# A new order table for 3779 steps on five engines: attention with exponential features, then a cosine feed-forward layer

## The chip, the core and the metric

The kernel runs on one core of a Trainium2 chip. The metric is the device time of one execution in microseconds (us). Engines are named as the profile names them: PE is TensorE (matmuls), PEld its weight loads, ACT is ScalarE, DVE is VectorE, POOL is GpSimd, SP is the queue that issues the transfers. L912 is line 912 of the kernel.

## The reference, cut to what matters

```python
def phi(x):                                   # q, k: 8 x 8 x 576 x 64; w_phi: 64 x 128
    proj = einsum('bhsd,df->bhsf', x, w_phi)
    proj = proj - max(abs(proj), axis=-1)
    return concatenate([exp(proj), exp(-proj)], axis=-1)
q_p, k_p = phi(q), phi(k)
kv  = einsum('bhsf,bhsd->bhfd', k_p, v);  z = sum(k_p, axis=2)
x   = einsum('bhsf,bhfd->bhsd', q_p, kv) / (einsum('bhsf,bhf->bhs', q_p, z)[..., None] + 1e-6)
h   = x.reshape(4608, 512) @ w_in             # w_in: 512 x 2048
out = (h * cos(h)) @ w_out                    # w_out: 2048 x 512
```

## The kernel before, in words

**Attention** (`attention`, L526) runs in 32 units, each of two heads. A unit projects q (L555, and L558 for the last 64 rows of both heads) and k (L601, L626) on PE. For q, ACT copies the result to SBUF (L566, L568), DVE takes the maximum over 32 x 32 blocks (L572, L580, L581), POOL spreads it (L586), DVE turns it back (L590), POOL subtracts (L594) and ACT takes the exponentials (L665). For k, DVE takes the maximum from PSUM (L639); in most units DVE negates it (L642) and ACT takes the exponentials with it as a bias (L659, eight instructions for a full half, two for the last rows); in the first units PE subtracts the maximum with one more matmul (L647), and ACT needs two instructions only (L656). PE then forms kv and z together (L705, L711), ACT copies them (L717), PE multiplies with the features of q (L740, L746), DVE divides (L752 to L767) and turns the result (L771), and SP stores it to DRAM (L781 the first 512 columns in four transfers, L777 the last 64). The turned tile `xt` has two buffers, so the turn of a unit waits until both stores of the unit two before it have landed.

**The feed-forward layer** (`visit`, L802) works on nine chunks of 512 tokens. A visit loads x (L825), splits it into a high and a low part (L49 on ACT, L54 on DVE) and forms, for a pair of 128 x 512 tiles of h at a time, x @ w_in on PE. Visits up to the ninth do this plainly (L960, 12 matmuls to a tile). Later ones use seven block products in place of eight (L912), with their sums made by DVE and ACT (L847, L924, L939, L943). From h on, the chain is the same: ACT copies out of PSUM (L967, L968) or scales (L982), DVE reduces the angle (L986), ACT takes the cosine (L990), DVE multiplies (L993), ACT and DVE split into high and low (L49, L54), and PE multiplies with w_out (L1009, L1010, L1011, three matmuls for a block of 128 tokens). The results leave through L1049, L1058, L1060 and the stores of L1069.

**The weights** (`convert`, L393) come as 64-bit words. For each of eight pairs of row blocks, ACT and DVE convert them early in the run (L415 to L462, and L49 and L54 for the parts), DVE makes four sums of blocks for the seven-product scheme in the same conversion (L470), and SP stores the parts to DRAM (L480), from where later visits load them again (L516). Exponentials and cosines need different tables on ACT, so each change between them stands as an ACT_TABLE_LOAD.

**What sets the order.** Every piece of work is a `Step` (L68) with an engine and a function that issues its instructions. There are 3779 of them: 958 on PE, 1040 on ACT, 1233 on DVE, 160 on POOL, 388 on SP. The list `ORDER` (L87) holds the numbers of all steps, and `plan` (L302) walks it once: the steps are issued in that order, each engine gets its own in that order, and the eight PSUM banks are given out on the way (a step that needs a bank takes the one whose last user stands earliest). An engine works its queue strictly in that order. A step waits for the steps that it depends on and for the last users of the bank or buffer that it takes over; the tables of costs (L85, L300) play no part any more when the kernel is issued.

Of the kernel before, what the change touches and what calls it, by code (L numbers as in the profile page):

```python
# [25 lines left out]
def phi_attention_then_cos_ffn(ctx: ExitStack, tc: tile.TileContext, qkT, vS, w_phi, w_in, w_out, out):  # L26
# [41 lines left out]
    class Step:  # L68
# [19 lines left out]
        0, 42, 1, 3, 1265, 2, 4, 5, 7, 44, 6, 8, 9, 59, 46, 17, 64, 10, 65, 11, 18, 19, 58, 68, 83, 23, 47, 24,  # L88
        43, 12, 27, 45, 20, 48, 124, 1266, 21, 16, 60, 22, 13, 62, 61, 14, 50, 25, 1267, 63, 26, 15, 49, 86, 30,
        28, 1268, 31, 66, 1269, 99, 1270, 67, 32, 51, 71, 1271, 84, 33, 29, 1284, 72, 103, 52, 1272, 73, 53, 85,  # L90
        140, 1273, 87, 88, 104, 57, 101, 89, 1280, 1281, 142, 100, 56, 102, 125, 108, 90, 165, 55, 141, 91, 143,
        107, 54, 144, 35, 74, 105, 69, 146, 1274, 1275, 34, 147, 1276, 106, 112, 92, 109, 1277, 70, 93, 36, 113,
        37, 38, 1278, 114, 94, 126, 150, 148, 181, 1279, 128, 127, 145, 39, 95, 129, 130, 185, 98, 182, 40, 75,
        149, 183, 97, 131, 76, 1285, 96, 132, 206, 166, 187, 153, 188, 133, 77, 134, 154, 111, 78, 1286, 115,
        168, 1287, 184, 110, 186, 79, 191, 1295, 1288, 167, 135, 222, 169, 247, 41, 170, 1289, 116, 171, 189,
        155, 137, 224, 117, 226, 156, 138, 190, 172, 136, 223, 80, 227, 1290, 139, 118, 81, 225, 151, 173, 209,
        174, 194, 152, 119, 175, 228, 207, 229, 1291, 195, 232, 230, 196, 120, 208, 1292, 248, 231, 263, 1506,
        210, 176, 288, 212, 157, 211, 1296, 213, 179, 158, 121, 178, 265, 235, 122, 177, 1511, 159, 160, 180,
        264, 192, 214, 236, 82, 1512, 237, 197, 269, 193, 215, 266, 289, 267, 216, 123, 161, 238, 1505, 268,
        271, 270, 217, 1507, 249, 272, 1297, 304, 251, 162, 219, 252, 250, 218, 306, 305, 163, 198, 253, 273,  # L100
        307, 221, 254, 1509, 199, 255, 220, 1513, 329, 233, 308, 276, 310, 311, 256, 234, 277, 1510, 200, 257,
        278, 314, 309, 1514, 1508, 312, 290, 201, 330, 1298, 240, 1299, 292, 1314, 239, 1300, 1515, 345, 293,
        1516, 279, 313, 1301, 291, 1517, 368, 347, 258, 1302, 294, 317, 348, 1303, 1518, 318, 353, 259, 202,
        349, 319, 260, 1528, 1304, 296, 261, 274, 350, 203, 262, 320, 354, 241, 204, 346, 1305, 385, 1537, 1519,
        242, 275, 1306, 164, 351, 1307, 352, 1529, 295, 384, 297, 355, 243, 298, 1538, 390, 332, 386, 331, 1530,
        1308, 244, 281, 1539, 245, 280, 387, 1309, 1531, 333, 299, 407, 335, 334, 358, 205, 1293, 1540, 336,
        303, 1520, 388, 1315, 300, 282, 283, 302, 1546, 1564, 337, 1312, 301, 246, 284, 369, 1521, 1310, 338,
        316, 285, 339, 1316, 315, 1541, 1317, 392, 1318, 370, 1319, 1522, 371, 372, 321, 389, 446, 391, 1523,
        373, 1563, 374, 322, 340, 287, 393, 286, 375, 424, 344, 1524, 323, 1547, 341, 1325, 376, 343, 324, 1320,
        423, 429, 325, 342, 394, 326, 357, 397, 377, 327, 1321, 1569, 356, 425, 378, 427, 359, 409, 1532, 1542,  # L110
        1567, 428, 1322, 398, 1525, 411, 410, 412, 1543, 1526, 1566, 1533, 430, 1565, 1548, 413, 361, 447, 432,
        1534, 1283, 1570, 485, 360, 1294, 379, 1527, 362, 383, 1535, 363, 1549, 415, 380, 1573, 1536, 1550,
        1326, 414, 382, 364, 1544, 381, 1574, 1551, 463, 1571, 1545, 1552, 468, 1572, 1553, 469, 1568, 433, 395,
        416, 426, 1554, 365, 417, 396, 1327, 1575, 1328, 1559, 472, 1560, 1329, 431, 1282, 1330, 448, 1331,
        1576, 462, 1561, 450, 502, 451, 466, 1562, 449, 1586, 408, 1577, 328, 467, 418, 366, 1578, 452, 1555,
        421, 454, 1332, 1344, 400, 1557, 524, 419, 367, 1587, 464, 420, 399, 1311, 453, 422, 436, 507, 1333,
        1621, 434, 1324, 1588, 435, 1334, 488, 1595, 1335, 465, 401, 471, 455, 508, 1336, 402, 456, 1337, 511,
        403, 487, 437, 457, 1596, 501, 489, 1579, 438, 470, 404, 459, 439, 505, 458, 405, 503, 460, 490, 475,
        440, 1338, 461, 441, 563, 442, 1323, 473, 504, 1339, 491, 527, 474, 486, 1604, 506, 493, 406, 443, 1580,
        1622, 492, 476, 444, 509, 1597, 494, 478, 1581, 1558, 495, 510, 477, 496, 540, 1605, 498, 526, 542, 500,  # L120
        479, 514, 1623, 480, 499, 1342, 481, 1598, 497, 482, 1589, 1599, 483, 528, 1582, 1590, 1627, 1606, 1583,
        515, 1591, 543, 541, 1556, 1584, 530, 1607, 1592, 1585, 1625, 546, 1608, 1593, 1600, 544, 1609, 545,
        1601, 529, 1594, 1624, 1345, 1626, 445, 532, 525, 1602, 564, 531, 1610, 1629, 1603, 1346, 1631, 547,
# [1027 lines left out]
```

## Time and profile before

| | us |
|---|---|
| three runs | 1038.51, 1039.48, 1040.59 |
| median | 1039.48 |
| the profiled execution, its own time | 1037.65 |
| its span (first to last instruction) | 1035.9 |
| PE busy in it | 1026.4 |
| ACT busy | 790.0 |
| DVE busy | 742.9 |

The time of an execution holds the span and some 1.75 us around it (1037.65 - 1035.9). The profiled execution lies 1.83 us below the median of the three runs. A view of the profile in windows gives the busy time of each engine between two marks, in us from the start of the span; the columns after the engines are the TensorE clock that was granted (1.00 is full), the share of the transfer engines that was busy, and GB/s. In the timeline a row gives the start, the length, the engine, the line and how many instructions are merged in it, and in square brackets how long the engine was idle just before and what ended that. Matmuls overlap, so the pitch of two rows is read from their starts. A step of fp32 data shows twice as many matmuls as the program issues.

### The profile page before, as it was taken

Reading aid. Unit: us, or ns where it says so; the run is one execution under the profiler, and the core shown is the slowest. Engines: PE = TensorE matmul, PEld = TensorE weight load, DVE = VectorE, ACT = ScalarE, POOL = GpSimd, SP = SyncE. Lnnn points to the kernel's source line nnn. Section 1 sums busy time; section 2 is a strip of 40 time slices with the busy share of each in tenths; the row PEclk is TensorE's granted clock in tenths of the full one; section 3 lists DMA queues with packets and bytes.
Section 4 is the critical chain, followed back from the end, with each engine's and each line's share of the span. In section 5 each row is a group of like instructions: output and inputs, shape, how many; then the busy total and the mean of one; then the engine's idle time right before and its main releaser. Section 6 shows DMA issues by size and latency. Waiting matters only on the chain.

```text
span 1035.9 us, 24223 instructions
## 1 busy us (share of the span) xinstructions
PE 1026.4 (99%) x9738; PEld 883.3 (85%) x9738; DVE 742.9 (72%) x1426; ACT 790.0 (76%) x1634; POOL 147.7 (14%) x231
## 2 busy tenths in 40 slices
PE   9998999999999999999999999999999999999998
PEld 6786788888878888988889898888899989989897
DVE  7998998999898877766677457686556475466544
ACT  6999999898777778787789958887778555455543
POOL 3342242201101001201112011132001000000000
PEclk9999999999999999999999999999999999999999
DMA  7676587247677644687336761567317655752852
GB/s 250 189 217 203 169 261 244 100 159 247 225 246 269 203 147 163 210 277 288 115 111 222 254 230 67 185 235 260 153 55 277 213 157 182 265 180 96 284 193 92
DMA packets 88768, 204.44 MB, mean 197 GB/s; under 512 B 20688, under 2 KB 42320, under 8 KB 84816
## 3 DMA queue, kind: packets, MB, share of 16 engines
q1 hardware_dynamic: 88512, 202.83, 57.9%
q8 instruction: 76, 1.25, 0.5%
q14 instruction: 36, 0.29, 0.1%
q10 hardware_dynamic: 144, 0.07, 0.0%
HBM read 154.63 MB, written 48.23 MB: 196 GB/s over the span
## 4 chain that ended last, share of the span: by engine, by line
PE 95%; DVE 3%; issue 1%; DMA 0%; SPq 0%; ACT 0%; DVEq 0%
PE bank L912 23%; PE bank L1009 13%; PE bank L1010 12%; PE bank L1011 12%; PE bank L960 12%; PE bank L705 6%; PE bank L740 6%; PE bank L555 3%; PE bank L601 3%; PE bank L711 1%; PE bank L647 1%; PE bank L558 1%; PE bank L626 1%; PE bank L746 1%; DMA wo_parts<-wo 0%
## 5 line engine op out<-in xcount | busy, mean ns | idle before, releaser
L1009 PE MATMUL bank<-wo,gh 128*128 128x512 f32 x576 | 229.5, 399 | 0.0
L1010 PE MATMUL bank<-wo,gh 128*128 128x512 f32 x576 | 225.3, 391 | 0.0
L1011 PE MATMUL bank<-wo,gl 128*128 128x512 f32 x576 | 224.6, 390 | 0.0
L924 ACT ACTIVATE hs<-bank 128x256 f32<-128x256 f32 x192 | 71.2, 389 | 92.7 <-PE bank L912 81.7
L594 POOL TENSOR_TENSOR pq<-pq,bq 128x288 f32<-128x288 f32 x128 | 114.2, 923 | 172.1 <-DVE bq L590 121.5
L986 DVE SCALAR_TENSOR_TENSOR g<-g,hs 128x512 f32<-128x512 int32 x144 | 98.2, 689 | 50.7 <-ACT g L982 47.6
L659 ACT ACTIVATE ek<-bank,mk 128x128 f32<-128x128 f32 x464 | 128.3, 420 | 5.4 <-DVE mk L642 5.1
L54 DVE TENSOR_TENSOR gl<-g,gh 128x512 fp32r<-128x512 f32 x144 | 100.4, 701 | 40.7 <-ACT gh L49 39.4
L1011 PEld LDWEIGHTS bank<-wo,gl 128*128 128x128 f32 x576 | 108.2, 188 | 23.8
L1009 PEld LDWEIGHTS bank<-wo,gh 128*128 128x128 f32 x576 | 108.4, 188 | 23.3 <-issue 2.2
L990 ACT ACTIVATE g<-g,halfpi 128x512 f32<-128x512 f32 x144 | 101.4, 719 | 30.4 <-DVE g L986 29.9
L912 PE MATMUL bank<-xh_t,wi 128*128 128x256 f32 x768 | 124.0, 284 | 0.4 <-issue 0.4
L1010 PEld LDWEIGHTS bank<-wo,gh 128*128 128x128 f32 x576 | 108.6, 188 | 18.2
L993 DVE TENSOR_TENSOR g<-hs,g 128x512 f32<-128x512 f32 x144 | 97.6, 689 | 31.7 <-ACT g L990 31.3
L49 ACT ACTIVATE gh<-g 128x512 fp32r<-128x512 f32 x144 | 91.5, 641 | 31.2 <-DVE g L993 16.2
L912 PEld LDWEIGHTS bank<-xh_t,wi 128*128 128x128 f32 x768 | 109.4, 191 | 6.4 <-issue 1.2
L586 POOL COPY m<-m 32x36 f32<-32x36 f32 x96 | 32.7, 341 | 469.4 <-DVE m L581 445.4
L912 PE MATMUL bank<-xh_b,wi 128*128 128x256 f32 x576 | 93.3, 284 | 0.0
L665 ACT ACTIVATE eq<-pq 128x576 f32<-128x576 f32 x128 | 81.3, 716 | 4.0 <-PE bank L740 2.5
L912 PEld LDWEIGHTS bank<-xh_b,wi 128*128 128x128 f32 x576 | 81.0, 191 | 2.8 <-issue 0.2
L982 ACT ACTIVATE g<-hs 128x512 int32<-128x512 f32 x96 | 60.2, 638 | 24.5 <-DVE hs L939 18.9
L912 PE MATMUL bank<-xl_t,wi 128*128 128x256 f32 x384 | 77.3, 283 | 0.0
(93 smaller groups left out, 1803.4 us busy)
## 6 DMA issues: line engine op xcount, KB each, us to landing
wi<-wi_parts SPq DMA_DIRECT2D x30, 1792.0 KB, 8.3
wo<-wo_parts SPq DMA_DIRECT2D x30, 1024.0 KB, 5.5
qk<-qkT SPq DMA_DIRECT2D x31, 640.0 KB, 5.3
x_raw<-xs SPq DMA_DIRECT2D x47, 256.0 KB, 4.8
vs<-vS SPq DMA_DIRECT2D x32, 325.0 KB, 4.8
wi_raw<-w_in SPq DMA_DIRECT2D x8, 1024.0 KB, 6.1
wo_raw<-w_out SPq DMA_DIRECT2D x8, 1024.0 KB, 6.2
xs<-xt SPq DMA_DIRECT2D x128, 64.0 KB, 3.4
```

Source lines behind the costliest of these rows:

```text
L49: ACT.activation(out=out, in_=in_, func=AF.Copy, scale=1.0)
L54: eng.tensor_tensor(out=out, in0=in_, in1=hi.bitcast(F32), op=ALU.subtract)
L594: qeng.tensor_tensor(out=d["pq"][:, c], in0=d["pq"][:, c], in1=d["bq"][:, c], op=ALU.subtract)
L659: ACT.activation(out=e[:, g, s * P:(s + 1) * P], in_=pk[:, g, :], func=AF.Exp, scale=1.0 - 2.0 * s, bias=d["lk" if s == 0 else "mk", i][:, ...
L912: PE.matmul(out=out, lhsT=w[:, part, block, j * P:(j + 1) * P], rhs=d[x, name][:, j * HC:(j + 1) * HC], start=start and k == 0, stop=k == ...
L960: PE.matmul(out=bank(b), lhsT=w[:, part, 2 * r + kt // 2, kt % 2 * P:(kt % 2 + 1) * P], rhs=d.get(("from", kt), d)[x, kt], start=(k == 0), ...
L986: DVE.scalar_tensor_tensor(out=g, in0=g.bitcast(I32), scalar=-TWO_PI, in1=m["hs", r], op0=ALU.mult, op1=ALU.add)
L990: ACT.activation(out=n["g"], in_=n["g"], func=AF.Sin, bias=halfpi, scale=1.0)
L993: DVE.tensor_tensor(out=n["g"], in0=m["hs", r], in1=n["g"], op=ALU.mult)
L1009: PE.matmul(out=a, lhsT=gh[:, t], rhs=w[:, 0, r], start=first, stop=False)
L1010: PE.matmul(out=a, lhsT=gh[:, t], rhs=w[:, 1, r], start=False, stop=False)
L1011: PE.matmul(out=a, lhsT=gl[:, t], rhs=w[:, 0, r], start=False, stop=last)
```

## The change

The change replaces the list `ORDER`. The list of steps, their functions, their dependencies and their buffers are the same; the new list holds the same 3779 numbers, and 3669 of its places hold another number than before. By the words that came with it, the table is from a search over four sets of transfer landing times at once; the sums of weight blocks in the conversions (L470), which these words name as well, stand in both kernels. Since banks are given out along the list, many steps use another PSUM bank than before.

```diff
     ORDER = [
-        0, 42, 1, 3, 1265, 2, 4, 5, 7, 44, 6, 8, 9, 59, 46, 17, 64, 10, 65, 11, 18, 19, 58, 68, 83, 23, 47, 24,
+        0, 4, 3, 5, 7, 8, 42, 6, 1, 44, 17, 18, 9, 45, 59, 1265, 46, 2, 10, 19, 23, 20, 58, 24, 47, 11, 12, 27,
...
-        3765, 3759, 3766, 3767, 3770, 3768, 3772, 3771, 3769, 3774, 3773, 3776, 3775, 3777, 3778,
+        3770, 3768, 3771, 3773, 3774, 3769, 3776, 3777, 3775, 3778,
     ]
```

Two places show what moves. The first is the DVE queue at the start of the program, before the change and after it; `mk` is the maximum of k over a bank, `m` and `bq` that of q. Before:

```order
L572 TENSOR_REDUCE m_127<-pq 128x18 x2
L639 TENSOR_REDUCE mk<-bank_74 128x1
L580 TENSOR_TENSOR m_150<-m_127 64x36
L581 TENSOR_TENSOR m_151<-m_150 32x36
L642 TENSOR_SCALAR mk<-mk 128x1
L639 TENSOR_REDUCE mk<-bank_75 128x4
L639 TENSOR_REDUCE mk<-bank_69 128x1
L642 TENSOR_SCALAR mk<-mk 128x1
L590 STREAM_TRANSPOSE bq<-m_151 128x1152
L639 TENSOR_REDUCE mk<-bank_76 128x4
```

And after:

```order
L572 TENSOR_REDUCE m_121<-pq 128x18 x2
L580 TENSOR_TENSOR m_150<-m_121 64x36
L581 TENSOR_TENSOR m_151<-m_150 32x36
L639 TENSOR_REDUCE mk<-bank_74 128x4
L639 TENSOR_REDUCE mk<-bank_76 128x1
L642 TENSOR_SCALAR mk<-mk 128x1
L590 STREAM_TRANSPOSE bq<-m_151 128x1152
L639 TENSOR_REDUCE mk<-bank_75 128x4
L639 TENSOR_REDUCE mk<-bank_69 128x1
```

The long transpose of L590 stood between the second and the third full maximum of k (banks 75 and 76 before); it now stands between the first and the second of them (banks 74 and 75).

PE takes up these maxima with L647, whose rows at the same place read, before:

```order
L558 MATMUL bank_72<-qk,wphi 128x128
L647 MATMUL bank_75<-mk,minus 128x512
L647 MATMUL bank_76<-mk,minus 128x512
L647 MATMUL bank_71<-mk,minus 128x512
L647 MATMUL bank_70<-mk,minus 128x512
```

And after:

```order
L647 MATMUL bank_74<-mk,minus 128x512
L601 MATMUL bank_71<-wphi,qk 128x128
L601 MATMUL bank_72<-wphi,qk 128x128
L601 MATMUL bank_71<-wphi,qk 128x128
L601 MATMUL bank_72<-wphi,qk 128x128
L601 MATMUL bank_71<-wphi,qk 128x128
L601 MATMUL bank_72<-wphi,qk 128x128
L601 MATMUL bank_71<-wphi,qk 128x128
L601 MATMUL bank_72<-wphi,qk 128x128
L647 MATMUL bank_75<-mk,minus 128x512
```

One whole projection of k (eight matmuls of L601) now stands between the first and the second of these subtractions, where the first two followed each other.

The third place is the SP queue near 85 us, in the stretch where attention, conversions and the first visits overlap. The numbers behind `xt` tell the units apart: xt_1308 before and xt_1250 after are the turned tile of one and the same unit, xt_1397 and xt_1372 that of the next. Before:

```order
L781 DMA xs_77<-xt_1308 32x4x128 x4
L777 DMA xs_tail_78<-xt_993 128x64
L781 DMA xs_77<-xt_1397 32x4x128 x4
L537 DMA qk_1448<-qkT 128x1280
L777 DMA xs_tail_78<-xt_1308 128x64
L480 DMA wo_parts0_98<-wo_728 128x1024
L825 DMA x_raw_1522<-xs_77 128x512
L480 DMA wi_parts1_91<-wi_1228 128x1024
L777 DMA xs_tail_78<-xt_1397 128x64
```

And after:

```order
L537 DMA qk_1378<-qkT 128x1280
L480 DMA wi_parts0_90<-wi_321 128x768
L777 DMA xs_tail_78<-xt_1250 128x64
L541 DMA vs1_89<-vS 128x650
L781 DMA xs_77<-xt_1250 32x4x128 x4
L480 DMA wi_parts0_90<-wi_321 128x768
L781 DMA xs_77<-xt_1372 32x4x128 x4
L480 DMA wi_parts1_91<-wi_1231 128x1024
L777 DMA xs_tail_78<-xt_1372 128x64
```

The last of the two stores that free a buffer of `xt` (xs_tail of xt_1308) stood behind the store of the next unit's tile; now both stores of a tile (xt_1250) stand ahead of it, and a load of v stands between them.

418 rows, old and new, of the table ORDER are left out of this document.

## Prediction

> **What bounds the kernel now.** I read the page first, then busy time by windows, then PE's waits, then the timeline where PE waits. The page gives the span and the engines:
>
> ```profile
> span 1035.9 us, 24223 instructions
> PE 1026.4 (99%) x9738; PEld 883.3 (85%) x9738; DVE 742.9 (72%) x1426; ACT 790.0 (76%) x1634; POOL 147.7 (14%) x231
> ```
>
> PE is busy for 1026.4 of 1035.9 us, and no step is added or taken away. An order can win only in the 9.5 us between, or where PE is busy but slow. The windows say where these lie:
>
> ```profile
> 0.00:66.00 66.00, 64.65 (x1092) 49.37 (x1092) 57.45 (x126) 54.95 (x109) 28.03 (x51) 1.00 0.70 221
> 66.00:113.00 47.00, 43.27 (x645) 33.97 (x642) 43.95 (x98) 45.43 (x114) 14.19 (x23) 0.96 0.62 191
> 113.00:165.00 52.00, 51.87 (x636) 42.78 (x635) 49.32 (x111) 51.84 (x111) 16.70 (x27) 1.00 0.69 221
> 165.00:400.00 235.00, 235.00 (x1575) 192.54 (x1574) 201.74 (x324) 197.31 (x357) 28.82 (x37) 1.00 0.62 208
> 400.00:1036.00 636.00, 631.60 (x5799) 564.61 (x5798) 390.42 (x770) 440.43 (x948) 59.96 (x95) 1.00 0.55 189
> ```
>
> After the lengths come PE, PEld, DVE and ACT. From 165 us to the end PE is idle for 4.4 us in all, most of it the last stores. From 66 to 113 us it is idle for 3.7 us, the granted clock is 0.96, and ACT is busy for 45.43 of 47 us. That is the one stretch with something to win. PE's waits name who ended them:
>
> ```profile
> PE bank L740 <- ACT ek L659: 2.7, 1, 2.7
> ...
> PE bank L705 <- ACT pq L566: 0.5, 1, 0.5
> ...
> PE bank L647 <- DVE mk L639: 0.2, 1, 0.2
> ```
>
> The largest is one pause ended by the exponentials of k on ACT. No transfer stands in PE's list: loads are hidden behind work, in 165 us and later as well. The pause in PE's timeline, and the clock after it (windows, TensorE clock third from the end):
>
> ```profile
> 94.16 0.49 PE L558 MATMUL bank<-qk,wphi 128*128 128x128 f32 x2
> 97.39 3.60 PE L740 MATMUL bank<-kv,eq 128*64 128x65 f32 x64 [2.75 <-ACT ek L659]
> ...
> 97.00:98.00 1.00, 0.61 (x14) 0.61 (x16) 0.97 (x2) 1.00 (x4) 0.00 (x0) 0.79 0.99 390
> 98.00:99.00 1.00, 1.00 (x24) 1.00 (x22) 0.90 (x2) 1.00 (x3) 0.00 (x0) 0.50 1.09 444
> 99.00:100.00 1.00, 1.00 (x24) 1.00 (x22) 1.00 (x4) 0.22 (x1) 0.00 (x0) 0.50 0.98 403
> 100.00:101.00 1.00, 1.00 (x25) 1.00 (x23) 1.00 (x2) 1.00 (x5) 0.00 (x0) 0.50 1.11 378
> ```
>
> Behind a pause of 2.75 us the clock fell to one half for some 3.4 us, which costs PE 0.21 + 3 x 0.5 = 1.7 us more. [...]
>
> **Term 1, the stretch that ACT limits.** From the end of one tile of h (L960) to the first matmul that waits for the last exponentials of this stretch, before has:
>
> ```profile
> 73.70:112.50 38.80, 35.10 (x534) 27.68 (x533) 35.85 (x86) 37.91 (x91) 13.27 (x21) 0.96 0.57 174
> ```
>
> ACT works 37.91 of 38.80 us: PE's loss here is ACT's work less PE's. PE is idle for 3.70 us and loses 1.7 to the clock, so its own work is about 38.80 - 3.70 - 1.7 = 33.4 us. In the new order the same kind of stretch, with the same last exponentials at its end, begins one step group earlier, at a projection of q (L555) that frees ACT. Counted from the two orders, ACT has in it the same groups as before and one half of exponentials of k (eight L659) and one weight part (L49, 128x1024) more, and one x part (L49, 128x512) less. PE has one tile of L960 and one step of L740 with L746 more, and three matmuls of L1009 to L1011 less. Pitches of these, from the starts of neighbouring rows:
>
> ```profile
> 78.33 2.23 ACT L659 ACTIVATE ek<-bank,mk 128x128 f32<-128x128 f32 x8
> 80.33 1.38 ACT L665 ACTIVATE eq<-pq 128x576 f32<-128x576 f32 x2
> ...
> 72.52 1.13 ACT L49 ACTIVATE wi<-wi_t 128x1024 fp32r<-128x1024 f32 x1
> 73.47 0.34 ACT L568 ACTIVATE pq<-bank 128x128 f32<-128x128 f32 x1
> ...
> 105.34 0.70 ACT L49 ACTIVATE xh_t<-x_raw 128x512 fp32r<-128x512 f32 x1
> 105.86 1.32 ACT L665 ACTIVATE eq<-pq 128x576 f32<-128x576 f32 x2
> ```
>
> ```profile
> 67.14 1.15 PE L740 MATMUL bank<-kv,eq 128*64 128x65 f32 x32
> 68.35 1.10 PE L740 MATMUL bank<-kv,eq 128*64 128x65 f32 x32
> ...
> 70.96 2.76 PE bank L960 x12
> ...
> 1022.30 0.39 PE L1009 MATMUL bank<-wo,gh 128*128 128x512 f32 x1
> 1022.98 0.39 PE L1009 MATMUL bank<-wo,gh 128*128 128x512 f32 x1
> ```
>
> ACT: 2.00 + 0.95 - 0.52 = 2.43 us more. PE: 2.76 + 1.21 - 0.68 = 3.29 us more. PE has 0.86 us more to do while it waits for ACT, so the loss falls by 0.9. The bounds: nothing, if these steps stand where PE waits anyway, and 1.8 us, if ACT's own idle time (38.80 - 37.91 = 0.89) goes too.
>
> **Term 2, ACT's idle time in that stretch.** Its cause can be followed on DVE, SP and ACT:
>
> ```profile
> 94.52 0.78 DVE L771 STREAM_TRANSPOSE xt<-rb 128x576 f32<-128x576 f32 x1 [1.55 <-DMA wo_parts<-wo]
> ...
> 85.55 3.43 SPq L781 DMA_DIRECT2D xs<-xt  x4
> 89.08 0.39 SPq L537 DMA_DIRECT2D qk<-qkT  x1
> 89.52 0.45 SPq L777 DMA_DIRECT2D xs_tail<-xt  x1
> ...
> 99.78 2.17 ACT L659 ACTIVATE ek<-bank,mk 128x128 f32<-128x128 f32 x8 [0.78 <-DVE mk L642]
> ```
>
> DVE stood 1.55 us before a turn (L771) until a transfer landed. That transfer must be a store that frees a buffer of `xt`: the xs_tail of two units back, which left SP only at 89.52, behind the four stores of the next tile, and 5 us before DVE went on. (The row names a weight store issued beside it.) DVE's delay then kept ACT waiting for 0.78 us, for L642. In the new order both stores of a tile stand ahead of the next tile's, so that they no longer wait for its turn. What they wait for instead is a load of v, queued ahead of one of them, which needs its buffer back from an earlier L705; that step stands one group of L601 (0.98), two steps of L740 (1.21 each) and one tile of L960 (2.76), over 6 us of PE work, ahead of the turn. So this wait should go, worth 0 to 0.8 us. In the same stretch two other halves of exponentials now stand closer behind their L642 on DVE than any did before, and can make ACT wait in turn. I take half: 0.4 us less.
>
> **Term 3, the start.** Between the first two full maxima of k DVE now has L639 for the tail, L642 and the transpose L590; PE has one projection (L601) and one L647 between the two matmuls that use these maxima.
>
> ```profile
> L590 DVE STREAM_TRANSPOSE bq<-m 128x1152 f32<-128x1152 f32 x32 | 43.8, 1368 | 1.8 <-POOL m L586 1.8
> L639 DVE TENSOR_REDUCE mk<-bank 128x4 f32<-128x512 f32 (+1 forms) x96 | 50.7, 543 | 14.7 <-PE bank L626 6.6 <-PE bank L601 5.7 <-ACT g L990 2.4
> ...
> 21.04 1.13 PE L555 MATMUL bank<-qk,wphi 64*128 64x512 f32 x4
> 22.00 1.06 PE L601 MATMUL bank<-wphi,qk 64*128 64x128 f32 x16
> 22.98 1.13 PE L647 MATMUL bank<-mk,minus 128*128 128x512 f32 x2
> 23.95 0.27 PE L626 MATMUL bank<-wphi,qk 128*128 128x128 f32 x1
> ```
>
> DVE needs about 1.37 + 0.54 plus some 0.3 for the small ones, 2.2 us; PE has 0.98 + 0.97, 1.95 us. PE waits 0.25 us longer here, and the old wait of 0.2 us for L639 stands where it did or goes: between 0.5 us lost and 0.2 won, I take 0.3 lost.
>
> **Term 4, changes of shape on PE.** PE's matmuls use the whole array, its upper rows (L555, L601: 64 rows) or half its columns (L705 to L746). From L555 to L601, both of the upper rows, the pitch is 0.96 us (21.04 to 22.00). From L555 to L740 it is 67.14 less the start of this row:
>
> ```profile
> 66.08 1.13 PE L555 MATMUL bank<-qk,wphi 64*128 64x512 f32 x4
> ```
>
> That is 1.06 us, so a change of shape costs 0.10 us. Counted from the orders there are 151 such changes before and 156 after: 0.5 us lost. With other pairs of neighbours it can be 0 to 1.5.
>
> **Term 5, the rest.** From 165 us on PE waits for nothing that the list shows, and the new order leaves the chains from L912 to L1009 as long in PE work as they were, except at the very end: behind the last L912 the new order has 8 double groups of L1009 to L1011 before the last tile's, where there were 10. Their 16 x 0.68 = 10.9 us of PE work now cover 12 single instructions of DVE (none longer than the 0.78 us of L771, 9.4 us at most) and the ACT instructions between them. That is cover still; for a wait in it I take 0.2 us lost, between 0 and 0.8.
>
> **The sum.** -0.9 - 0.4 + 0.3 + 0.5 + 0.2 = -0.3 us. Against the profiled execution that is 1037.65 - 0.3 = 1037.35; the median of the runs lies 1.83 above it, so 1039.2 us for the median. About 0.2% (2.1 us) is what a measurement of this kernel can tell from no change; this is none.
>
> **Rivals.**
>
> *Faster: the stretch falls to ACT's floor.* Term 1 then gives 1.8 us with ACT's idle time in it, the start wait of 0.2 goes, and the changes of shape cost nothing more: 1.8 + 0.2 and 0.5 more if PE's own 33.4 us shrink where it need not start again behind a wait: 2.5 us, 1037.0. For it speaks that the cause of DVE's wait is moved, and that, by the same counts and pitches, PE falls behind ACT by about 1 us at each of five places in the new order and not by 2.75 at one, so the clock may stay whole. Against it: ACT, not PE, limits that stretch, so a whole clock mostly buys waiting. Chance 0.30.
>
> *Slower: the half clock on the path.* The new stretch ends with L740 waiting for eight L659, and behind it ACT's lead over PE grows again. A pause at that place as long as 2.75 us would halve the clock when PE is the limit, and its 1.7 us would not be hidden behind ACT. With Term 2 at nothing, and 0.8 at the end: -0.9 + 1.7 + 0.3 + 0.5 + 0.8 = +2.4, 1041.9. It decides at the length of the longest pause: some 2.7 us does it, as above; five pauses of 1 us don't. [...] Chance 0.23.
>
> *Nothing moves.* The terms cancel within 2.1 us: my forecast, 0.47.
>
> **How the numbers follow.** The range takes in 1037.0 and 1041.9 with 0.8 to 0.9 us around them for the bounds of Terms 3 to 5: 1036.2 to 1042.8. Faster 0.30, within 0.2% 0.47, slower 0.23.
>
> **What would show it.** Right: PE idle 2 to 4 us between 66 and 113 us, ACT busy there above 95%, no wait of DVE's L771 on a transfer near 94 us, PE's wait for L639 0.3 to 0.6 us in all, nothing new after 165 us. A window at half clock behind a pause under 2 us, or waits of PE after 165 us of over 1 us, above all for a transfer (loads of wi or wo landing late), would make it wrong.

## The result, and the profile after

The new table is slower. The median of the kernel after is 1046.15 us (6 executions, 1042.82 to 1048.23) against 1038.47 us before (6 executions, 1037.48 to 1040.59): a ratio of 1.0072, 95% interval 1.0052 to 1.0092, some 7.5 us. The prediction was 1039.2 us in a range of 1036.2 to 1042.8. The profiled execution of after was its fastest, 1042.82 us with a span of 1041.1 us and a granted clock of 1.000; the five others had a clock of .998 or .996. That spread, 5.4 us against 3.1 before, belongs to the result. One execution in experiment 2 took 1439.68 us at a granted clock of .655 and is left out of its median.

The page gives PE 1026.9 us of 1041.1: PE is idle for 14.2 us, where it was 9.5. So 4.7 of the 5.2 us between the two spans are waits. Before's 1026.4 us of work held 1.7 us of half clock that this execution of after has not, so at full clock PE's own work grew as well, by some 2.2 us (1026.9 - 1026.4 + 1.7); 4.7 + 2.2 - 1.7 gives the 5.2. The same windows as for before (lengths, then PE, PEld, DVE, ACT, POOL, TensorE clock, DMA):

```profile
66.00:113.00 47.00, 42.26 (x675) 33.88 (x671) 44.51 (x101) 45.91 (x114) 14.95 (x25) 1.00 0.69 220
113.00:165.00 52.00, 51.65 (x633) 42.62 (x632) 47.69 (x104) 50.82 (x110) 16.34 (x25) 1.00 0.56 174
165.00:400.00 235.00, 234.27 (x1572) 192.12 (x1571) 205.80 (x325) 198.88 (x354) 31.99 (x35) 1.00 0.61 208
400.00:1036.00 636.00, 633.57 (x5802) 564.71 (x5801) 392.36 (x776) 442.16 (x952) 59.34 (x98) 1.00 0.55 191
```

From 66 to 113 us PE is now idle for 4.74 us instead of 3.73, but at full clock; before lost 1.7 us to half clock there. Between 165 and 400 us, where PE had no idle time at all, it has 0.73. PE's list of waits names the largest loss:

```profile
PE bank L912 <- DMA wi<-wi_parts: 2.2, 1, 2.2
PE bank L740 <- ACT pq L566: 1.4, 1, 1.4
...
PE bank L1009 <- ACT ek L659: 0.9, 1, 0.9
PE bank L647 <- DVE mk L639: 0.8, 1, 0.8
PE bank L601 <- ACT pq L566: 0.7, 1, 0.7
PE bank L740 <- ACT ek L659: 0.7, 1, 0.7
PE bank L740 <- ACT kv L717: 0.6, 1, 0.6
```

There is one long wait, and it is for a transfer; PE's list in before had no wait for a transfer. Below it the one pause of 2.7 us for ACT has become several of 0.5 to 1.4. PE's timeline at the long one:

```profile
832.69 0.39 PE L1011 MATMUL bank<-wo,gl 128*128 128x512 f32 x1
835.29 0.74 PE L912 MATMUL bank<-xh_b,wi 128*128 128x256 f32 x4 [2.21 <-DMA wi<-wi_parts]
```

PE stops at the first use of weights that step 3131 loads (a reload of wi, L516). What SP did ahead of that load, in after's timeline of SP (start, length, issuing line):

```profile
807.68 0.32 SPq L516 DMA_DIRECT2D wo<-wo_parts  x1
808.05 0.53 SPq L516 DMA_DIRECT2D wi<-wi_parts  x1
808.63 9.55 SPq L781 DMA_DIRECT2D xs<-xt  x8
818.22 9.29 SPq L834 DMA_DIRECT2D x_raw<-xs_tail  x16
827.62 0.52 SPq L516 DMA_DIRECT2D wi<-wi_parts  x1
```

and the same load in before:

```profile
806.35 0.52 SPq L516 DMA_DIRECT2D wi<-wi_parts  x1
806.93 9.01 SPq L834 DMA_DIRECT2D x_raw<-xs_tail  x8
816.09 0.52 SPq L516 DMA_DIRECT2D wi<-wi_parts  x1
```

PE's first use of that load in before:

```profile
829.66 0.65 PE L912 MATMUL bank<-xh_b,wi 128*128 128x256 f32 x4
```

Between the two wi loads before had 8 transfers, after has 24: eight stores and sixteen loads, 18.8 us of SP's time. The load goes out at 827.62 instead of 816.09 us. By the trace's landing times it landed at 835.25 us, and PE goes on at 835.29; in before it landed at 825.79 and was first used at 829.66, 3.9 us later. SP's own waits between 800 and 840 us say why the eight stores took 9.55 us:

```profile
SPq L516 <- PE bank L1011: 7.6, 1, 7.6
SPq L781 <- DMA wi<-wi_parts: 5.1, 1, 5.1
```

First the wo load stood 7.6 us at the head of the queue, until PE gave its buffer back. Then the eighth transfer behind the first wi load had to wait 5.1 us until that load had landed: every transfer signals its landing on one of eight semaphores, which the program uses in turn, and each one waits until the transfer before it on its semaphore has landed (smallest distance 0.02 us; last section).

**The theory (T).** One reload of weights, queued too late on SP, lands in the microsecond of its first use. The wait varies from execution to execution, and when it is long enough, half clock follows. **Rivals.** R1: the spread and the loss come from the stretch to 113 us, through half clock there. R2: other work, longer chains or new waits elsewhere. R3: all of it lies behind 685 us. Later forecasts add R4 (the DMA engines, not the queue), G (PE's idle time brings half clock), and S and C for what is left once the load is early (the front of the program, or chains behind it).

### The profile page after: what moved, and what is told of

Its sections match the earlier page's. It is cut to its first block, busy times and chain, and to the rows that moved or that the text cites. A ratio compares the mean times of both kernels' runs of the same rounds, so it can differ in the third digit from the quotient of the medians.

```text
span 1041.1 us, 24198 instructions
## 1 busy us (share of the span) xinstructions
PE 1026.9 (99%) x9738; PEld 881.6 (85%) x9738; DVE 749.1 (72%) x1426; ACT 792.5 (76%) x1636; POOL 148.5 (14%) x231
## 4 chain that ended last, share of the span: by engine, by line
PE 82%; DVE 7%; ACT 6%; DMA 2%; issue 1%; SPq 1%; DVEq 0%; ACTq 0%
PE bank L912 22%; PE bank L1009 12%; PE bank L1011 12%; PE bank L1010 11%; PE bank L960 9%; PE bank L705 4%; PE bank L740 4%; PE bank L601 2%; PE bank L555 2%; ACT ek L659 2%; DMA xs<-xt 1%; PE bank L647 1%; PE bank L711 1%; ACT eq L665 1%; DMA wi<-wi_parts 1%
## 5 line engine op out<-in xcount | busy, mean ns | idle before, releaser
L1009 PE MATMUL bank<-wo,gh 128*128 128x512 f32 x576 | 229.8, 399 | 0.9 <-ACT ek L659 0.9
L1009 PEld LDWEIGHTS bank<-wo,gh 128*128 128x128 f32 x576 | 108.5, 188 | 25.1 <-issue 3.2
L912 PE MATMUL bank<-xh_t,wi 128*128 128x256 f32 x768 | 124.6, 285 | 0.2 <-ACT ek L659 0.2
L993 DVE TENSOR_TENSOR g<-hs,g 128x512 f32<-128x512 f32 x144 | 99.6, 697 | 26.0 <-ACT g L990 25.7
L912 PEld LDWEIGHTS bank<-xh_t,wi 128*128 128x128 f32 x768 | 108.7, 191 | 7.1 <-ACT hs L924 1.2
L912 PE MATMUL bank<-xh_b,wi 128*128 128x256 f32 x576 | 93.8, 285 | 2.2 <-DMA wi<-wi_parts 2.2
L912 PEld LDWEIGHTS bank<-xh_b,wi 128*128 128x128 f32 x576 | 81.0, 191 | 6.2 <-DMA wi<-wi_parts 2.6
L912 PE MATMUL bank<-xl_t,wi 128*128 128x256 f32 x384 | 77.3, 283 | 0.0
L740 PEld LDWEIGHTS bank<-kv,eq 128*64 128x64 f32 x2048 | 64.5, 138 | 13.1 <-ACT pq L566 3.0
```

What stands on the lines that cost most here:

```text
L740: PE.matmul(out=ps[64 * h:64 * h + 64, 65 * g:65 * g + 65], lhsT=d["eq", j][:, n, c:c + 64], rhs=d["kv"][:, 2 * n + j, :], start=h not in ...
L912: PE.matmul(out=out, lhsT=w[:, part, block, j * P:(j + 1) * P], rhs=d[x, name][:, j * HC:(j + 1) * HC], start=start and k == 0, stop=k == ...
L993: DVE.tensor_tensor(out=n["g"], in0=m["hs", r], in1=n["g"], op=ALU.mult)
L1009: PE.matmul(out=a, lhsT=gh[:, t], rhs=w[:, 0, r], start=first, stop=False)
```

## The experiments

All were compared with before on the same chip; "ratio" is to before.

**1. The kernel after, again**, no edit.

> The kernel after, unchanged, for more executions and a second trace. Its profiled execution (span 1041.1 us, time 1042.82, granted clock 1.000) was the fastest of six; the other five, at 1045.77 to 1048.23 us, had a granted clock of .996 or .998. Theory T (late loads): the wi load of step 3131, queued on SP behind 24 other transfers, lands in the microsecond of its first use; in slow executions PE waits there for over the 2.2 us of the profiled one, and half clock follows. A trace at 1045 to 1048 us then shows a PE wait of 3 us or more for wi or wo at 700 to 1005 us, with a half-clock window behind it. Rival R1 (spread from the ACT-limited stretch): it shows the half clock between 85 and 112 us, behind a PE pause for ACT, and the transfer wait at 835 us stays near 2.2. Rival R2 (other work): no half clock, and the time lies spread over PE's steps. Median by all: 1044 to 1048 us.

Median 1045.70 us (6 executions, 1042.65 to 1047.54), ratio 1.0066 (1.0051 to 1.0081). The profiled execution took 1045.65. PE's row at the place, and the windows behind it (PE, PEld, DVE, ACT, POOL, clock):

```profile
836.65 0.74 PE L912 MATMUL bank<-xh_b,wi 128*128 128x256 f32 x4 [3.57 <-DMA wi<-wi_parts]
```

```profile
837.00:838.00 1.00, 1.00 (x8) 1.00 (x7) 0.00 (x0) 0.00 (x0) 0.00 (x0) 0.65 0.94 359
838.00:839.00 1.00, 1.00 (x7) 1.00 (x6) 0.00 (x0) 0.00 (x0) 0.00 (x0) 0.50 0.87 237
```

All other waits are within 0.1 us of those of the first trace. The wait for wi is 3.57 instead of 2.21 us, the clock is one half from 837.30 on for 3.41 us, and the span is 1043.9 instead of 1041.1 us: 1.36 + 1.7 = 3.1 us come from this one place, a little more than the 2.8 us between the spans. That is T's picture. R1 does not show: there is no half clock in the stretch to 113 us in either trace of after. Of these six executions the two with clocks of .999 and 1.000 are the two shortest, 1043.07 and 1042.65.

**2. The same load earlier.** Two versions: four stores behind the previous wi load, and directly behind it.

```
-    ]
+    ]; ORDER.remove(3131); ORDER.insert(ORDER.index(1146) + 1, 3131)
```

```
-    ]
+    ]; ORDER.remove(3131); ORDER.insert(ORDER.index(3100) + 1, 3131)
```

> The kernel after with one DMA issue moved: the wi load of step 3131 right behind the store of step 1146, 20 transfers earlier on SP. T: the PE wait at 835 us (2.2 us in the profiled execution) is gone; a fast execution has a span of 1038.5 to 1039.5 us, and the median falls by 2.2 to 5 us, to 1041 to 1044 us, as the half clock behind that wait goes with it. R1: the fastest execution falls by 2.2 us, but the median by no more (about 1044), since half clock still comes in the stretch to 112 us. R2: the wait is replaced by another of its size; median 1045 to 1047.

> The kernel after with the wi load of step 3131 at the first place that its buffer allows, right behind the wi load of step 3100; SP then waits there some 5 us for the buffer, and the 8 stores and 16 loads behind it go out later. T: no PE wait for wi at 835 us, as with the load four stores further down (1043.5 us median, 1041.6 lowest). The trace of that one held a PE pause of 1.95 us at 75 us that the profile puts down to no wait, with half clock behind it; after's own traces have none. If that pause comes by chance, it is absent here or in part of the executions, and the lowest time is 1039.5 to 1040.5 us; if it belongs to these programs, lowest 1041.5. Rival: the stores and loads held back make a new wait, 1043 to 1046.

The first: median 1043.48 us (5 executions, 1041.56 to 1044.02), ratio 1.0041 (1.0028 to 1.0054). The second: 1041.31 us (5 executions, 1040.94 to 1044.29), ratio 1.0046 (1.0034 to 1.0059). The wait for wi is gone in both; in the second, SP issues both wi loads together and then the rest:

```profile
809.04 5.84 SPq L516 DMA_DIRECT2D wi<-wi_parts  x2
814.93 8.95 SPq L781 DMA_DIRECT2D xs<-xt  x8
823.92 8.05 SPq L834 DMA_DIRECT2D x_raw<-xs_tail  x16
```

The load now lands some 9 us (first version) and 10 us (second) before its first use, and the stores and loads held back make no new wait of its size. With the two runs of after at 1.0072 and 1.0066, moving one DMA issue is worth about 0.0026, 2.7 us, in both versions alike. (The two were measured on different chips, so the ratios are compared and not the medians.) T had said 2.2 to 5 us; the fastest span of the first version, 1039.8 us, lies just above its 1038.5 to 1039.5. R2 falls for this part of the loss: no other wait takes the place. R1 does not fall as clearly: beside experiment 1, on the same chip, the first version's median is lower by 2.2 us and, with 1043.48, near R1's 1044. Its trace has half clock in the stretch to 113 us too, but not behind a pause for ACT: the pause stands in the middle of a run of 64 matmuls, and after's two traces did not have it.

```profile
75.49 0.57 PE L705 MATMUL bank<-vs,ek 128*64 128x65 f32 x11 [1.95 <-issue]
```

The second has it too, with 1.13 us and no half clock behind it; its lowest time, 1040.94 us, lies between the forecasts for a pause by chance and for one in every execution. The pause is taken up at the end.

**3. The same load later, in the kernel before.** The other direction: before with step 3131 moved behind the wo load of step 3070.

```
-    ]
+    ]; ORDER.remove(3131); ORDER.insert(ORDER.index(3070) + 1, 3131)
```

> The kernel before with the same wi load (step 3131) put late: right behind the wo load of step 3070, that is behind a store and eight x loads. It then issues at about 824 to 827 us instead of 816.1, lands 8 to 9.5 us later, and its first use stood at 829.7 us. T: PE waits 2.5 to 6 us there for wi, with half clock behind it when over about 2.7, and the median is 1041 to 1046 us (2.5 to 7.5 over before). R1 and R2 have the price of a late load at its wait alone, with nothing behind it: 1040.5 to 1042. If the load takes less time with fewer transfers ahead of it, no wait: 1038.5.

Median 1045.15 us (5 executions, 1044.04 to 1045.19), ratio 1.0062 (1.005 to 1.0074), in T's range and above the 1040.5 to 1042 of R1 and R2. One moved DMA issue makes before as slow as after. SP, then PE:

```profile
818.71 4.55 SPq L834 DMA_DIRECT2D x_raw<-xs_tail  x8
825.48 0.34 SPq L516 DMA_DIRECT2D wo<-wo_parts  x1
825.86 0.52 SPq L516 DMA_DIRECT2D wi<-wi_parts  x1
```

```profile
835.59 0.77 PE L912 MATMUL bank<-xh_b,wi 128*128 128x256 f32 x2 [4.89 <-DMA wi<-wi_parts]
```

The load goes out at 825.86, lands at 835.45 us, and PE waits 4.89 us with half clock from 835.34 on. 4.89 + 1.7 = 6.6 us, against 6.4 us between the medians (elsewhere this execution lost 1.7 us at 72 us to a late load of x, and had no half clock near 97 us, which saved as much). T is shown in both directions.

**4. All 60 reloads at the first place that their buffers allow**, right behind the last user of the buffer.

```
-    ]
+    ]; [(ORDER.remove(a), ORDER.insert(ORDER.index(b) + 1, a)) for a, b in ((2185, 2165), (2216, 2198),
...
+    (3649, 3616), (3618, 3647), (3680, 3678))]
```

> The kernel after with all 60 reloads of wi and wo issued right behind the last user of their buffer, as the kernel before has nearly all of them; every other step in the order of after. T: no PE wait for a transfer is left behind 400 us, executions agree within 2 us, and the median is 1039.5 to 1041.5 us: after's own 1042.8 less 2.2, and what is left over 1038.5 are shape changes (+0.8) and steps behind 165 us (about +2) less 1.3 in the ACT-limited stretch. R1: the spread stays, median 1043 to 1045. R2: loads at their earliest place delay stores and loads of x behind them on SP; new PE waits for x, median 1044 to 1047.

Median 1083.47 us (6 executions, 1078.81 to 1089.23), ratio 1.0434: 45 us slower than before and 37 slower than after. All three forecasts missed. "Earlier" is not the remedy. PE's waits, and SP's:

```profile
PE bank L1011 <- DVE gl L54: 7.8, 2, 7.4
PE bank L1009 <- DVE o L1049: 7.8, 1, 7.8
PE bank L555 <- DMA qk<-qkT: 3.9, 1, 3.9
PE bank L740 <- DVE o L1060: 3.4, 1, 3.4
```

```profile
SPq L516 <- PE bank L912: 189.2, 25, 18.0
SPq L516 <- PE bank L1011: 166.0, 23, 13.3
```

The same two rows of SP in after:

```profile
SPq L516 <- PE bank L912: 126.3, 19, 18.0
SPq L516 <- PE bank L1011: 118.6, 16, 13.3
```

SP issues in the table's order. A reload at the head of its queue waits for PE to give the buffer back, and everything behind it waits too: 355 us of such waits instead of 245. The sum alone does not make a kernel slow: before has 261 us of it. What counts is what stands behind the waiting load. Stores of o, loads of qk and of v then come late, and PE waits for those. Of the rivals R2 named this mechanism (new waits behind held-back transfers) but not its size. Half clock came on top, 27.3 us of it in all, 13.7 us lost (a granted clock of .987 over 1083.1 us). Counted from the two orders, before has no other SP step between the last user of the buffer and the reload in 44 of 60 cases, after in 15. So before issues most of its reloads as early as this and is the faster table: early loads go with its other steps and not with after's, though this run does not tell with which of them. In after's order the right place for a load is bounded on both sides.

**5. The same load on another queue**, at its place in the table.

```
-            SP.dma_start(out=tile, in_=parts)
+            (ACT if step is steps[3131] else SP).dma_start(out=tile, in_=parts)
...
-        w_ready[me] = [Step("SP", 0.5 if kind == "wi" else 0.38, load, w_stored[me], take=[slot], kind="r.load", pipe=5.3 if kind == "wi" else 2.9)]
+        w_ready[me] = [step := Step("SP", 0.5 if kind == "wi" else 0.38, load, w_stored[me], take=[slot], kind="r.load", pipe=5.3 if kind == "wi" else 2.9)]
```

> The kernel after with the wi load of step 3131 issued from ACT's queue instead of SP's, at its place in the table; its bytes, its buffer and everything else stay. Theory T (the load is late because 24 transfers stand ahead of it in SP's queue, and SP issues no further while eight are under way): it issues where ACT passes that place, at 815 to 823 us instead of 827.6, lands 8 to 10 us later, and PE does not wait for it at 833 us. Lowest time about 1041, median 1041 to 1043 us, as with the load moved up on SP (1041.3). Rival R4 (the DMA engines are busy with the 24 transfers, whichever queue holds the load): it still lands at 833 us or later, PE waits 1 us or more, median 1043.5 to 1046.

Median 1042.76 us (11 executions, 1041.88 to 1045.18), ratio 1.004 (1.0027 to 1.0053): as with the load moved up on SP. But the way was another than T said:

```profile
827.90 0.59 ACTq L516 DMA_DIRECT2D wi<-wi_parts  x1
828.59 0.39 ACT L924 ACTIVATE hs<-bank 128x256 f32<-128x256 f32 x1 [5.17 <-PE bank L740]
834.02 0.74 PE L912 MATMUL bank<-xh_b,wi 128*128 128x256 f32 x4 [1.17 <-DVE rb L765]
```

This execution ran 3.2 us behind after's at this place (after a pause of 2.22 us at 76 us and half clock behind it, at a granted clock of .998; PE's step with the wo load of step 3008 begins at 829.88 instead of 826.63), so 827.90 is 824.65 in after's time: 3.0 us earlier than on SP, not 4.6 to 12.6. ACT idled for 5.17 us around the issue: the load went out at 827.90, right behind the landing of an x load of SP's at 827.88, the transfer before it on the same semaphore. The transfer itself took 8.2 us, between the 7.6 and 8.5 us on SP in the two traces of after. The load was 1.5 us early at its use; PE waited 1.17 us a little earlier, for DVE, which no trace of after has, so ACT's stop seems to have come back to PE by way of DVE. R4 falls as put, since PE does not wait for the load, but T's "SP's queue" was too narrow: the transfers ahead hold up the load on another engine's queue as well, through the eight semaphores that both queues share, and that engine with it.

**6. The two tables joined.** After's first 685 us and then before's order, and the reverse. In this and the next two experiments the new table is written as an expression; in the run it stands as a list of numbers.

```
-    ORDER = after
+    ORDER = after[:2613] + [x for x in before if x not in after[:2613]]
```

```
-    ORDER = after
+    ORDER = before[:2604] + [x for x in after if x not in before[:2604]]
```

> One table of two: the first 2613 places of after (to 685 us), and the steps that are left in the order of before. By the steps' starts in the two profiled executions, without the half clock that before had in its own (1.7 us): after's first part costs 0.2 us more up to 30 us, 0.6 to 66, 0.4 to 113, 0.5 to 165, 2.3 from there to 600, and about 0.5 of shape changes, together 4.5. Theory T (the late wi load of step 3131 is one part, longer chains and shape changes up to 600 us the other): span about 1038.7 us, median 1040 to 1041.5, no PE wait for a transfer at 830 us. Rival R3 (the whole loss lies behind 685 us, and what the trace shows ahead of it is noise of one execution): median 1038.3 to 1039.

> The other way round: the first 2604 places of before (to 680 us), and the steps that are left in the order of after. T: PE waits 2 to 4 us for wi at 830 to 837 us as in after, with half clock behind it when it is over 2.5 or so; median 1041 to 1043.5 us. R3: the same loss as after, 1045 to 1046.5. If the wait for wi needs the transfers that after's first part has shifted, it is gone here: 1038.5 to 1039.

After first: median 1042.35 us (5 executions, 1041.77 to 1045.56), ratio 1.0053 (1.0041 to 1.0065). Before first: 1045.14 us (1044.47 to 1047.57), ratio 1.0082 (1.007 to 1.0094). R3 falls: with before's order behind 685 us, over half of the loss stays, where R3 had 1038.3 to 1039 (the second median, 1045.14, lies in R3's range, but the first does not). The second shows the late load again, without after's first part, and four of its five executions have a granted clock of .997 or .998. (The fifth, the trace, records a granted clock of .95 from 7 us on, with matmuls of L1009 as long as before's between 500 and 800 us, 404 ns against 403.)

```profile
PE bank L740 <- ACT ek L659: 2.7, 1, 2.7
PE bank L912 <- DMA wi<-wi_parts: 2.7, 1, 2.7
```

The two do not add up to after (0.53 + 0.82 against 0.69%), since the joins bring waits of their own (0.58 us at 691 us in the first; 1.0, 0.8 and 1.0 at 303, 686 and 692 us in the second), and the first again has the pause at 76 us, 1.95 us, with half clock from 78.06. Both medians lie above what T forecast, 1040 to 1041.5 and 1041 to 1043.5.

**7. The front and the back, without the late load.** After's first 113 us and then before's; before's first 109 us and then after's, with step 3131 early.

```
-    ORDER = after
+    ORDER = after[:505] + [x for x in before if x not in after[:505]]
```

```
-    ORDER = after
+    ORDER = before[:496] + [x for x in after_3131_early if x not in before[:496]]
```

> The first 505 places of after (to 113 us) and the steps that are left in the order of before. What is open is the 2.5 to 4.5 us that after keeps over before once its wi load is early. Theory S (front): the first 113 us hold part of it: 0.2 up to 30 us, 0.6 to 66, 0.4 in the stretch as against before without its half clock, and a PE pause at 75 us, put down to issue, of 1.1 to 2.2 us, which stood in six of eight traces that have after's order there and in none of before's; with half clock behind it in some executions. Median 1.5 to 3 us over before of the same comparison, and the pause in the trace. Rival C (chains): the front costs nothing against before, whose own pause at 95 us is halved in most executions; median within 0.8 us of before.

> The other way round: the first 496 places of before, and the steps that are left in the order of after with the wi load of step 3131 early (behind that of 3100). Theory C: PE's short waits for DVE and ACT at 157, 235, 557 and 583 us (together 2.1 us more than before's) and about 0.5 of shape changes stay; median 2 to 3.5 us over before of the same comparison. Theory S: under 1.5 us over before. A new wait where the orders join, in the trace at 100 to 130 us, would be told by its row and taken off.

Front: median 1040.89 us (12 executions, 1039.38 to 1043.78), ratio 1.0023 (1.001 to 1.0035). Back: 1040.92 us (12 executions, 1039.35 to 1046.53), ratio 1.0025 (1.0011 to 1.0039). PE's waits in the back kernel:

```profile
PE bank L740 <- ACT ek L659: 2.8, 1, 2.8
PE bank L558 <- ACT pq L566: 1.6, 1, 1.6
...
PE bank L601 <- ACT pq L566: 0.7, 1, 0.7
...
PE bank L1011 <- DVE gl L54: 0.4, 1, 0.4
```

The waits at 159 (0.40), 237 (0.68) and 559 us (0.19) are those of after at 158, 235 and 558; the join brings none. So C's forecast for the back kernel holds, 2 to 3.5 us: 2.4 us over before come from behind the join. The three waits are 1.27 us of them; that the rest is changes of shape and slower steps is argued, not shown. C's forecast for the front kernel, within 0.8 us of before, fails. The front kernel has two waits that neither parent has, 1.00 and 0.85 us at 121 and 129 us, at the join; an estimate of some 0.5 us of its 2.4 is left for the front itself. Its clock was .999 or 1.000 in all twelve executions: before's half clock at 97 us is saved, and more than lost again. Theory S had 1.5 to 3 us for this kernel, and 2.4 lies in it, but not for its reasons: most of it is the join, and the pause at 75 us was absent from the trace. For the back kernel S had under 1.5 us, which fails.

**8. The stretch alone.** Before with after's order for places 291 to 505 only (62.5 to 113 us).

```
-    ORDER = before
+    first = before[:291]
+    first += [x for x in after if x not in first][:214]
+    ORDER = first + [x for x in before if x not in first]
```

> The kernel before with the order of after in the ACT-limited stretch alone: places 291 to 505 (62.5 to 113 us). The prediction's terms 1 and 2 gave this stretch -1.3 us (ACT idles less), half clock left as it was. The two profiled executions have it 1.3 us shorter in after between 66 and 113 us, but before's held a half-clock window that costs 1.7 us, so that without it the stretch would be 0.4 longer. As predicted: ACT idles less than 1 us in it, median 1037 to 1037.5. By the trace: its longest PE pause is 1.4 us instead of 2.75, no half clock behind it, median 1037.2 to 1038.5, and executions of before that have full clock too agree with it. Rival: joining the orders brings a new pause, 1038.5 to 1040.

Median 1042.32 us (6 executions, 1041.40 to 1045.84), ratio 1.0052 (1.0039 to 1.0065). It is inconclusive for the stretch: the join makes a load of qk late, and the two waits at the join that the front kernel had come again, here at 123 and 131 us.

```profile
PE bank L601 <- DMA qk<-qkT: 2.1, 1, 2.1
PE bank L740 <- ACT pq L566: 1.4, 1, 1.4
...
PE bank L1011 <- DVE gl L54: 1.0, 1, 1.0
...
PE bank L558 <- DVE o L1060: 0.9, 1, 0.9
```

What it does show is that the longest wait for ACT is 1.4 us in place of 2.7, without half clock behind it, as the trace forecast.

**9. PE's idle time before the half clock.** Before, with four matmuls added in the 2.75 us pause whose results nobody reads; nothing that the kernel computes is changed.

```
-            PE.matmul(out=bank(qb[2])[:, 0:P], lhsT=wphi, rhs=d["qr"][:, CT:CT + P], start=True, stop=True)
+            PE.matmul(out=bank(qb[2])[:, 0:P], lhsT=wphi, rhs=d["qr"][:, CT:CT + P], start=True, stop=True); [PE.matmul(out=bank(qb[2])[:, P:512], lhsT=wphi, rhs=d["qr"][:, 0:384], start=True, stop=True) for _ in range(4 if u == 9 else 0)]
```

> The kernel before with four matmuls added whose results nobody reads: right behind the 128x128 matmul at 94.2 us, into unused columns of its own bank, 1.6 to 1.7 us of PE in the 2.75 us pause that follows. In the traces so far half clock came in windows of 3.41 us on one grid for each execution, behind a window in which PE idled 1.8 us or more (1.81, 1.95, 2.02, 2.73, 2.75, 2.76, 3.4), and not behind one of 1.71, 1.58 or less (one of 2.02 did without). Theory G (that idle share decides): the pause is 1.0 to 1.4 us, no execution has half clock at 97 us, nearly all show a clock of .999 or 1.000, and the median is 1.2 to 1.7 us below that of before in the same comparison (about 1036.6 for 1038.2). Rival (the wait for ACT, not PE's idle time, goes with half clock, or the added matmuls hold up ACT's reading of the bank): same median as before within 0.5 us, or up to 1.7 longer.

Median 1038.13 us (11 executions, 1036.28 to 1039.35) against 1038.96 for before (22 executions): ratio 0.9986, interval 0.9975 to 0.9996. That is 0.8 us, where G had forecast 1.2 to 1.7; both lie in the interval, 0.4 to 2.6 us. Nine of the eleven have a clock of .999 or 1.000, against three of the 22 of before. PE's timeline at the old pause:

```profile
94.90 3.07 PE L558 MATMUL bank<-qk,wphi 128*128 128x128 f32 x10
98.16 1.04 PE L740 MATMUL bank<-kv,eq 128*64 128x65 f32 x28 [0.19 <-ACT ek L659]
```

The added matmuls took 2.8 us, more than the 1.7 planned, and filled the pause to 0.19 us; L740 starts 3.26 us behind the first L558, where it was 3.23, so ACT was not held up. Theory G holds for the clock: with PE's idle time filled, half clock is gone from nine of eleven executions, and work of no use in that time wins about 0.14%, at the edge of what the runs can tell. This version beats both kernels, by little.

## Why the prediction was wrong, point by point

- **What bounds the kernel.** Right for before, and it hid the danger: "No transfer stands in PE's list: loads are hidden behind work" was true, but with little to spare, which PE's list cannot show. The load of experiment 3 had 3.9 us; the tightest in that trace, a wi load, landed at 914.22 us and was used at 914.46, 0.24 us later, and a wo load had 0.64. The spare time of a load is read from its landing and its first use, not from a list of waits.
- **Term 5 is the step that failed**: "From 165 us on PE waits for nothing that the list shows, and the new order leaves the chains from L912 to L1009 as long in PE work as they were". It took 0.2 us, between 0 and 0.8. It followed chains over PE, ACT and DVE and left out SP, whose order the same table sets. The late wi load alone is 2.2 to 3.6 us in the two traces, with 1.7 of half clock in one of them, and some 2.7 us of the median by experiment 2. The chains did not hold either: PE has new waits of 0.35, 0.72 and 0.19 us at 158, 235 and 558 us, and the back kernel puts what lies behind 113 us, the late load apart, at 2.4 us.
- **Terms 1 and 2**, the stretch: -0.9 and -0.4. The mechanism of Term 2 was right: DVE's L771 no longer waits near 94 us, ACT's 0.78 at that place is gone, and ACT is busy for 45.91 of 47 us (97.7%). But the term's own doubt came true as well: ACT waits for another L642, 0.28 us at 67 us and 0.75 at 75 us, so little was won. And PE's idle time there rose from 3.73 to 4.74 us instead of falling by 1.3. So Term 1, that PE's new work would fill its waits for ACT, failed in its sign: PE now pauses at six places from 88 to 110 us, 0.5 to 1.4 us each, where it had 2.75 us at one and 0.5 or less at three. The stretch is still 1.3 us shorter between the two traces (expected text of experiment 8), which is what the two terms add up to, but that is luck: 1.7 us of it are half clock, and without that the stretch is 0.4 us longer. What the stretch did win, 1.7 us of half clock, was named by the faster rival, without a price, and not by the forecast. The front kernel is not faster than before for it.
- **Term 3**, the start: 0.3 us lost. PE's wait for L639 rose from 0.2 to 0.8, so it is 0.6, just above the bound of 0.5.
- **Term 4**, changes of shape: 0.5 us lost. An estimate from the medians of before's own neighbours, pair by pair, has the new sequence of PE's steps 0.8 us longer; within its bounds.
- **The median over the profiled execution**: 1.83 us was carried over from before. For after it is 3.3, since the wait for wi and the half clock behind it differ from execution to execution.
- **The rivals.** "Slower" had half clock as its mechanism, which was right, at the end of the stretch, which was wrong: it came at 837 us behind a transfer. Its test, the length of the longest pause, does not hold either (last section). The signs named for a wrong forecast were the ones that came: "waits of PE after 165 us of over 1 us, above all for a transfer (loads of wi or wo landing late)". They were worth a rival of their own.

**What stays open.** The parts come to 2.7 us for the load, 2.4 for the back and some 0.5 for the front, 5.6 of 6.9 to 7.5 us, each known to about 1.3 us; the pause at 75 us may be in the rest, and was not settled.

## What to carry to other kernels

When an order is changed, follow each load's place on the queue that issues it: count the transfers ahead of it since its buffer came free, and the time left between landing and first use. A load that lands with less to spare than its time varies can cost its wait and, when the wait is long enough, half clock behind it (here 3.57 us of waiting did, and 2.21 did not). Issuing everything as early as possible is no cure on a queue that works in order: a load that waits for its buffer there holds up whatever stands behind it (355 us of such waits in experiment 4, against 245).

## What the runs showed of the hardware that was not expected

**Eight transfers under way.** In the traces of before and after, none of 517 transfers each starts before the eighth ahead of it has landed (smallest distance 0.02 us, ten to twelve within 0.06 us), while counted to the seventh ahead 38 and 24 do. This is the program's doing: the transfers use eight semaphores in turn (517 of 517 in each trace), and none is issued before the one ahead of it on its own semaphore has landed. In experiment 5 the load on ACT's queue shares a semaphore with an x load from SP that landed at 827.88 us, and goes out at 827.90; there one transfer did start before the eighth ahead of it had landed, but none before the last of its own semaphore. Whether the chip would let more than eight run, no run here shows.

**Half clock lasts 3.41 us, and not every long pause brings it.** In before's trace the granted clock is one half for 3.413 us from 97.58 us on, and again from 1036.25 us on, behind the last instruction, 275 such lengths later; in the second trace of after it is one half for 3.41 us from 837.30 us on. Half clock came with pauses of 1.95 us (experiment 2, the first version, and experiment 6, after first), 2.22 (experiment 5), 2.75 (before), 3.57 (experiment 1) and 4.89 (experiment 3). It did not come with pauses of 1.13 (experiment 2, the second version), 2.08 (experiment 8), 2.21 (the first trace of after), 2.76 (experiment 3, at 99.6 us) and 2.77 us (the back kernel). So the length of a pause alone does not decide. An estimate from these traces: cut into stretches of 3.413 us, counted from a start of half clock, before's trace has all 2.75 us of its pause in the one stretch ahead of half clock, and the first trace of experiment 6 has 1.8 us of its 1.95 there (pause from 74.52 to 76.47 us, half clock from 78.06 on). The pauses of 2.21 us in after (counted from 1042.24 us, where its clock falls behind the last instruction) and of 2.76 us in experiment 3 (counted from 835.34) lie across two stretches, 0.94 and 1.27 us in one case and 1.21 and 1.55 in the other. One stretch of experiment 4 with some 2.0 us of idle time, not followed by half clock, does not fit. If the place of a pause decides in this way, that would explain why before, with one pause of 2.75 us, has executions with half clock and a few without (three of 22 show .999 or 1.000 in the comparison of experiment 9); no run tried it.

**A pause of PE put down to no wait.** Five of nine traces with after's order between 66 and 76 us show PE stopped for 1.13 to 2.22 us near 75 us, inside a run of 64 small matmuls, with everything they need long there; one more shows 0.17, after's own two and the front kernel's none, and none of the five traces with before's order there does. In after the trace's 16 KB instruction transfers come at 66.2, 70.7 and 74.7 us, in the first version of experiment 2 at 66.5, 73.1 and 78.2. The same goes for the rest: the second of the three comes at 71.8 to 74.1 us in the five traces with the pause, and at 70.5 to 70.7 in the three without. That PE had run out of instructions is a guess from these times; it was not tried.
